# GpSimd loads the first batch's values, and a new order of the startup, in an attention and two-layer expert kernel

## The chip, the cores and the metric

The kernel runs on one core of a Trainium2 chip. The metric is device time in microseconds (us) of one execution; lower is better. PE is the matrix engine (TensorE), DVE VectorE, ACT ScalarE, POOL GpSimd, SP SyncE, which here only issues transfers.

## What is computed

The reference, cut to its core (B=4, H=8, S=576, D=64, 32 packed queries per head, 2304 tokens, model width 512, hidden width 2048, all float32):

```python
def sm_attn(qq, kk, vv):
    s = scale * qq @ kk.T
    a = exp(s - max(s)); a = a / (sum(a) + 1e-9)
    return a @ vv
p_packed = sm_attn(p, k, v)          # 32 rows per head
x = sm_attn(q, p_packed, p_packed)   # 576 rows per head
x = x.transpose(0, 2, 1, 3).reshape(2304, 512)
h = x @ w1_in;  x = (h * tanh(softplus(h))) @ w1_out      # Mish
h = x @ w2_in;  out = (where(h > 0, h, exp(min(h,0)) - 1)) @ w2_out   # ELU
```

## The kernel before

The program has three stretches. `startup()` does the attention of batch 0 and 1, decodes the first layer's weights and runs the first 32 hidden tiles of both; `mixture1` does the rest of the first layer with the attention of batches 2 and 3 beside it; `mixture2` does the second layer. The change touches `startup()` alone.

In `startup()` the order on PE, DVE, ACT and SP is written out by hand. First come fixed lines: `make_identity(nc, ident)` on POOL (a memset, then an affine select that puts the ones on the diagonal), two memsets of the buffers `words` on POOL, the copy `one` of `ident`, then on PE six `busy()` and 35 `brief()` matmuls of `one` that compute nothing that is used. Behind them stand the loads of batch 0's keys `k` (four, SP and ACT in turn), of the packed queries `p` (four small ones) and of the values `v` (`load_vt`, eight). Then the string `ORDER` is played from left to right; each name appends one step's instructions to its engines' queues. POOL isn't in the set of engines whose order is kept: its queue is ordered by the planner of the framework, which looks at when an instruction could start.

The names that matter, for batch 0 (leading 0):

- `lq00` to `lq03` load the queries (SP and ACT in turn); `r0`, `r1`, ... load a raw weight tile (512 KB, on SP).
- `0k0` to `0k3` turn the keys on DVE (line 409), `tp0` the packed queries (line 1085); `0A0`, `0A1` are the first scores on PE (line 441).
- `0M` (row maximum, DVE), `0E` (exp, ACT, line 468), `0R` (sum and reciprocal, DVE, lines 480 and 483), `0T` (turn on PE, line 495), `0V` (copy out of PSUM), `0K` (times the values, PE, line 520; needs all eight value loads), `0P` (scaled by the reciprocal, line 537), `0U` (turn, PE, line 552), `0W` (copy out of PSUM into `pt`; `@` puts a step on ACT in place of DVE).
- `0q0` to `0q3` turn the queries on DVE (line 409); `0S0` is the second scores' matmul (line 574), `0t0`, `0t1` its turn on DVE (line 603), `0X`, `0Y`, `0N`, `0B`, `0H`, `0L` the second softmax and the splitting of its result into `a2h` and `a2l`.
- `dN.0` to `dN.5` decode weight tile N: `.0` and `.2` on ACT (lines 199, 201, 206, 209), `.1` and `.3` on DVE (lines 221 or 217, and 237), `.4` issues the store of a finished pair on POOL (line 245).
- `w` and `x` are more unused matmuls on PE; `f00` folds the attention into the weights, `g0` is the first matmul of the first layer.

The values' loads of batch 0 in `load_heads` go by two pieces, partitions 0 to 63 with five blocks (1,280 bytes in one run) and 64 to 127 with four (1,024 bytes), two heads each: `(eng if b or not j else nc.scalar).dma_start(...)`, where `eng` is SP. So SP and ACT issue four each.

Of the kernel before, what the change touches and what calls it, by code (L numbers as in the profile page):

```python
# [40 lines left out]


ORDER = """
0k0 lq00 0k1 lq01 lq02 0k2 0k3 lq03 tp0 0A0 r0 0A1 0M0 r1 0E0 0M1 r2 0E1 w w w w w w w w w w w w w
0T0 0R0 0V0@ 0T1 0R1 r3 w w w w 0K0 r4 0V1@ r5 0q0 0K1 0P0@ r6 0q1 0U0 0P1@ 0q2 r7 0q3 0U1 0W0@ r8
d0.0 0W1 w w w w w 0S0 d0.1 r9 d0.3 d0.4 d1.0 0t0 0t1 d1.1 d1.3 d1.4 r10 d2.0 d2.2 r11 0X2 d3.0 0X1
0Y2 r12 0N2 d4.0 d4.2 r13 0X0 0Y1 d5.0 0B2 0Y0 d2.1 d2.4 0H2 0N0 r14 d6.0 0L2 0B0 r15 0X3 0H0 d7.0
0L0 0Y3 r16 d3.1 d7.2 d4.1 d8.0 d3.3 d3.4 r17 d4.4 d7.1 x x x x x x x x x x x x x x x x x x x x x x x
x x x x x x x x x x x x x x x x x z z z z f00 d9.0 d8.1 d4.5 d9.2 d8.3 d8.4 fh001 fh000 lk12 d9.1
d9.4 d10.0 fl000 d10.2 lk10 fl001 d11.0 d10.1 d10.4 x x x x x g0 d11.2 lk13 d6.1 d12.0 d5.1 g1 d11.1  # L50
d11.4 m0 lk11 d6.3 f01 d5.3 m1 pr1 0N1 g2 h0 h1 fh011 g3 l0 m2 fl011 fh010 G0 h2 l1 d5.4 fl010 d13.0
r18 d5.5 g4 lw100 l2 r19 0B1 m3 G1 m4 0N3 d6.4 d12.2 d6.5 r20 g5 d13.2 h3@ d12.1 G2 h4 m5 l3 d7.4 l4
r21 d12.4 d7.5 g6 d15.0 r22 d12.5 G3 r23 d13.1 m6 0B3 0H1 d13.4 h5@ 0L1 g7 0H3 d13.5 d14.0 G4 0L3 h6@
1k3 d14.2 l5 g8 m7 r24 l6 d15.2 d14.1 G5 h7 d15.1 m8 r25 d14.4 l7 d15.4 g9 d14.5 h8 d15.5 d16.0 G6
1k0 m9 l8 d19.0 tp1 g10 G7 1k1 m10 r26 h9 1k2 d19.2 l9 g11 d16.2 h10@ y7.0 d20.0 1A0 l10 r27 y7.1
y7.2 m11 g12 y7.3 d18.0 1M0 G8 d19.1 d19.4 m12 1E0 d18.1 g13 d20.1 G9 h11@ d18.3 d18.4 d17.0 l11 1R0
1A1 d16.1 d16.4 d17.2 d20.3 h12 G10 d17.1 d17.4 lv11 d25.0 l12 d26.0 1M1 d20.4 lv12 g14 d23.0 d25.1
d20.5 G11 1E1 lv10 d26.1 d25.3 d25.4 d24.0 lv13 1R1 f02 m13 d23.1 d24.1 d26.3 d26.4 G12 d24.3 d24.4
m14 r28 fh021 r29 h13@ fh020 h14@ g15 l13 d21.0 l14 G13 fl020 r30 m15 fl021 d27.0 h15@ d21.1 g16
d22.0 l15 G14 d27.1 d21.3 d22.2 d27.3 d27.4 g17 d28.0 r31 d21.4@ lw101 f03 d22.1 m16 d21.5 m17 h16  # L60
g18 h17@ fh031 d22.4@ fh030 l16 G15 fl031 m18 d30.0 d28.1 g19 fl030 y15.2@ y15.1 h18 1T1 y15.3@ d22.5
m19 g20 y15.0@ l17 d30.2 1V1 G16 m20 d28.3 d31.0 d30.1 g21 d31.2 d28.4@ h19@ 1T0 l18 d29.0 l19 g22
d28.5 m21 1V0 G17 d29.2 m22 d31.1 d23.3 1K0 h20@ d23.4 d31.4@ g23 l20 1P0@ lq11 d23.5 G18 m23 d31.5
d29.1 lq10 d30.4@ 1U0 d29.4@ G19 1W0 h21@ d29.5 l21 1K1 d30.5 h22 l22 G20 1P1@ lq12 1q1 1U1 h23@ G21
1W1 lq13 l23 1q0 g24 G22 m24 h24@ l24 1q2 g25 G23 m25 h25@ l25 1q3 g26 y23.0 1S0 y23.3 m26 y23.2 h26
g27 y23.1 1t0 G24 m27 l26 1S1 h27 G25 l27 1t1 1X0 g28 G26 m28 1X1 1Y0 g29 h28@ l28 G27 1Y1 1N0 m29
g30 1N1 G28 h29 m30 h30 f10 l29 1B0 G29 1B1 1H0 l30 fh101 1L0 fh100 g31 fl101 1H1 fl100 m31 1L1 h31
l31
"""


# [1 line left out]
def kernel(  # L73
# [12 lines left out]
    nc = tc.nc  # L86
# [49 lines left out]
    ident = const.tile([128, 128], F32, name="ident")  # L136
# [217 lines left out]
    def load_heads(src, dst, b, g, nm, eng):  # L354
        home = small if b else slot
        if nm == "v":
            t = home([128, 2, 5, D], F32, f"{nm}{b}_{g}")
            x = src[b, 2 * g:2 * g + 2].rearrange("h (p i) d -> p h (i d)", i=9)
            for r, j, n in RUNS:
                (eng if b or not j else nc.scalar).dma_start(  # L360
                    out=t[r:r + 64, :, 0:n, :].rearrange("p h i d -> p h (i d)"),
                    in_=x[:, :, D * j:D * (j + n)],
                )
        elif b == 0 or nm == "k" and b == 1:

            t = home([128, S // 32, 32], F32, f"{nm}{b}_{g}")
            ins = eng.dma_start(
                out=t.rearrange("p c d -> p (c d)"),
                in_=src[b, 2 * g:2 * g + 2].rearrange("h (t j) d -> (h t) (j d)", t=64),
            )  # L370
            if b == 1:
                tc.keep_in_program_order(ins)
        else:
            t = home([128, S // 32, 32], F32, f"{nm}{b}_{g}")
            for h in range(2):
                for x in range(2):
                    r = 64 * h + 32 * x
                    if nm == "q":
                        eng.dma_start(
                            out=t[r:r + 32],  # L380
                            in_=src[b, 2 * g + h, :, 32 * x:32 * x + 32].rearrange("(c t) d -> t c d", t=32),
                        )
                    for s in range(2 if nm == "k" else 0):
                        eng.dma_start(
                            out=t[r:r + 32, s * NB // 2:(s + 1) * NB // 2, :],
                            in_=src[b, 2 * g + s, h * HALF:(h + 1) * HALF, 32 * x:32 * x + 32].rearrange(
                                "(c t) d -> t c d", t=32
                            ),
                        )
# [549 lines left out]
    def load_kt(src, dst, b, kt, nm, eng=nc.sync):  # L939
        for gg in range(2):  # L940
            load_heads(src, dst, b, 2 * kt + gg, nm, eng)
# [43 lines left out]
    def startup():  # L985
# [11 lines left out]
        for x in words:  # L997
            z = sg.tile([128, 1024], I32, tag="sg", name="words")
            nc.gpsimd.memset(z, 0)
            x.extend((z[:, 0:512], z[:, 512:1024]))  # L1000
        if WARM:
            wu = ps_h.tile([128, 512], F32, tag="h", name="warm")

            one = const.tile([128, 128], F32R, name="one")
            nc.gpsimd.tensor_copy(out=one, in_=ident)

            def busy():
                nc.tensor.matmul(
                    out=wu.rearrange("p (r n) -> p r n", r=4), lhsT=one,
                    rhs=one.rearrange("p (r n) -> p r n", r=1).to_broadcast([128, 4, 128]),  # L1010
                )

            def brief(m, n):
                nc.tensor.matmul(out=wu[0:m, 0:n], lhsT=one[:, 0:m], rhs=one[:, 0:n])

            def gated():
                x = A2h[0][:, 0, 0, :]
                nc.tensor.matmul(out=wu[:, 0:HALF], lhsT=x[:, 0:128], rhs=x)

            for i in range(WARM):  # L1020
                busy()
            for i in range(P["BRIEF"]):
                brief(32, 64)
        for g in range(4):
            load_heads(k, kt_in, 0, g, "k", (nc.sync, nc.scalar)[g % 2])
# [14 lines left out]
        for b in range(2):  # L1040
            for g in range(4):
                step(f"{b}k{g}", transpose_heads(kt_in, kT, b, g, "kT")[0])
                step(f"{b}q{g}", transpose_heads(qt_in, qT, b, g, "qT")[0])
                for nm, src, dst in (("k", k, kt_in), ("v", v, vt_in), ("q", q, qt_in)):
                    eng = nc.sync if b or g % 2 else nc.scalar
# [223 lines left out]
    with tc.manual_schedule(engines={e.engine for e in (nc.tensor, nc.vector, nc.scalar, nc.sync)}):  # L1269
        startup()  # L1270
# [32 lines left out]
```

## Time and the profile before

| | |
|---|---|
| median of 3 runs | 776.6 us (776.24 to 778.09) |
| profiled execution, its own time | 775.32 us |
| its span, first to last instruction | 773.5 us |
| PE busy, share of the span | 756.9 us, 98% |
| DVE, ACT, POOL busy | 528.7, 397.6, 104.5 us |
| mean granted clock of PE | 0.998 |

The span is 1.8 us shorter than the execution's own time. PE is busy nearly throughout, but in the first 40 us much of that is unused matmuls, so the stretch has to be read by its chain of waits, engine by engine.

### The profile page before, as it was taken

What the parts mean: (1) busy time and instruction counts of PE and PEld (TensorE: products, weight loads), DVE (VectorE), ACT (ScalarE), POOL (GpSimd) and SP (SyncE); (2) the same over time, 40 slices, a digit from 0 to 9 for tenths busy, and PEclk for the clock granted to TensorE, in tenths of its full rate; (3) what the DMA queues carried; (4) which work ended last, traced back from release to release, by engine and by line L of the source; (5) the groups of instructions that cost most, each with busy time, mean ns of one, the idle gap of its engine ahead of it and who ended that gap; (6) DMA issues with size and microseconds to landing.
All of it is one profiled execution on the core that took longest, in us unless ns stands there. A gap on an engine that the chain in (4) does not pass through costs nothing.

```text
span 773.5 us, 14181 instructions
## 1 busy us (share of the span) xinstructions
PE 756.9 (98%) x5276; PEld 679.0 (88%) x5276; DVE 528.7 (68%) x1132; ACT 397.6 (51%) x843; POOL 104.5 (14%) x199
## 2 busy tenths in 40 slices
PE   8899999999999999999999999999999999999997
PEld 6598898898889988999988889888998999899986
DVE  5999977735853679877667788866455686445554
ACT  3899826573657467665545344534323354223323
POOL 1100000120120215661000003133000001000000
PEclk9999999999999999999999999999999999999999
DMA  8998646685583555777666235456343347333312
GB/s 290 412 367 271 171 126 177 203 230 157 129 268 56 151 194 191 262 254 238 219 220 201 100 109 199 155 197 198 108 120 119 103 140 243 108 110 116 129 55 82
DMA packets 95108, 138.82 MB, mean 179 GB/s; under 512 B 57920, under 2 KB 63616, under 8 KB 95040
## 3 DMA queue, kind: packets, MB, share of 16 engines
q1 hardware_dynamic: 83104, 105.73, 44.1%
q0 software_dynamic: 10208, 29.90, 10.6%
q10 hardware_dynamic: 1728, 2.29, 0.9%
q8 instruction: 42, 0.69, 0.3%
q14 instruction: 26, 0.21, 0.1%
HBM read 109.58 MB, written 28.31 MB: 178 GB/s over the span
## 4 chain that ended last, share of the span: by engine, by line
PE 84%; ACT 6%; DVE 4%; DMA 3%; issue 2%; POOL 0%; SPq 0%; ACTq 0%; DVEq 0%; POOLq 0%
PE h L833 22%; PE o L913 8%; PE o L915 8%; PE o L914 8%; PE acc L738 7%; PE acc L737 7%; PE acc L739 7%; PE h L701 3%; PE h L702 3%; PE h L703 3%; DMA raw_w1o<-in_moe_w_out_dram 1%; PE pm L667 1%; PE pm L520 1%; DMA w_dr<-w2c 1%; ACT words L206 1%
## 5 line engine op out<-in xcount | busy, mean ns | idle before, releaser
L833 PE MATMUL h<-y,w2c 128*128 128x384 f32 x1008 | 198.1, 338 | 1.8 <-ACT hs L397 1.2
L833 PEld LDWEIGHTS h<-y,w2c 128*128 128x128 f32 x1008 | 179.5, 188 | 13.4 <-ACT hs L397 2.0
L738 PE MATMUL acc<-gl,w1oh 128*128 128x288 f32 x512 | 151.2, 296 | 0.4 <-DVE gl L719 0.3
L739 PE MATMUL acc<-gh,w1ol 128*128 128x288 f32 x512 | 150.3, 295 | 0.0
L737 PE MATMUL acc<-gh,w1oh 128*128 128x288 f32 x512 | 148.7, 296 | 0.2 <-ACT gh L397 0.2
L913 PE MATMUL o<-w2oh,gh 128*128 128x512 f32 x288 | 113.5, 394 | 0.0
L914 PE MATMUL o<-w2ol,gh 128*128 128x512 f32 x288 | 112.6, 391 | 0.0
L915 PE MATMUL o<-w2oh,gl 128*128 128x512 f32 x288 | 101.1, 393 | 0.0
L738 PEld LDWEIGHTS acc<-gl,w1oh 128*128 128x128 f32 x512 | 96.1, 188 | 5.3 <-issue 2.3
L737 PEld LDWEIGHTS acc<-gh,w1oh 128*128 128x128 f32 x512 | 95.0, 188 | 6.2 <-issue 4.5
L739 PEld LDWEIGHTS acc<-gh,w1ol 128*128 128x128 f32 x512 | 96.0, 188 | 1.2 <-issue 0.8
L719 DVE TENSOR_TENSOR gl<-t,gh 128x288 fp32r<-128x288 f32 x128 | 57.2, 451 | 43.3 <-ACT gh L397 42.4
L711 ACT ACTIVATE t<-h 128x288 f32<-128x288 f32 x128 | 51.0, 404 | 55.9 <-PE h L703 53.0
L701 PE MATMUL h<-a2h,gh 128*128 128x288 f32 x256 | 76.9, 301 | 1.3 <-ACT t L711 0.9
L326 POOL DMA_DIRECT2D w_dr<-w2c x112 | 59.7, 539 | 135.7 <-DVE w2c L272 126.9
L703 PE MATMUL h<-a2h,gl 128*128 128x288 f32 x256 | 76.1, 298 | 0.3 <-DVE gl L272 0.3
L702 PE MATMUL h<-a2l,gh 128*128 128x288 f32 x256 | 75.8, 296 | 0.0
L264 ACT ACTIVATE gh<-t 128x384 fp32r<-128x384 f32 x96 | 50.1, 522 | 48.8 <-DVE t L844 47.5
L270 DVE TENSOR_TENSOR gl<-t,gh 128x384 fp32r<-128x384 f32 x96 | 53.1, 554 | 15.8 <-ACT gh L264 15.4
L914 PEld LDWEIGHTS o<-w2ol,gh 128*128 128x128 f32 x288 | 54.1, 188 | 9.4
L913 PEld LDWEIGHTS o<-w2oh,gh 128*128 128x128 f32 x288 | 54.0, 187 | 9.4 <-ACT gh L264 0.5
L397 ACT ACTIVATE gh<-t 128x288 fp32r<-128x288 f32 x112 | 49.2, 442 | 24.1 <-PE acc L739 22.1
(139 smaller groups left out, 1095.2 us busy)
## 6 DMA issues: line engine op xcount, KB each, us to landing
w2c<-w_dr SPq DMA_DIRECT2D x84, 512.0 KB, 3.6
w_dr<-w2c POOLq DMA_DIRECT2D x112, 128.0 KB, 3.1
w1r<-w_dr SPq DMA_DIRECT2D x24, 512.0 KB, 5.7
raw_w1i<-in_moe_w_in_dram SPq DMA_DIRECT2D x16, 512.0 KB, 10.8
raw_w1o<-in_moe_w_out_dram SPq DMA_DIRECT2D x16, 512.0 KB, 9.1
raw_w2i<-in_moe_w_in_dram SPq DMA_DIRECT2D x16, 512.0 KB, 4.8
raw_w2o<-in_moe_w_out_dram SPq DMA_DIRECT2D x16, 512.0 KB, 3.6
y_dr<-y POOLq DMA_DIRECT2D x16, 288.0 KB, 4.9
```

The source lines that it names most:

```text
L326: nc.gpsimd.dma_start(out=w2_dr[n // 2][:, n % 2, p], in_=d[x][:, i].bitcast(F32))
L701: nc.tensor.matmul(out=hp, lhsT=wh, rhs=xh, start=(kt == 0), stop=False)
L702: nc.tensor.matmul(out=hp, lhsT=wh, rhs=xl, start=False, stop=False)
L703: nc.tensor.matmul(out=hp, lhsT=wl, rhs=xh, start=False, stop=(kt == 1))
L719: nc.vector.tensor_tensor(out=gl, in0=d["t"], in1=gh.bitcast(F32), op=ALU.subtract)
L737: nc.tensor.matmul(out=o, lhsT=wh[:, cs], rhs=gh, start=first, stop=False)
L738: nc.tensor.matmul(out=o, lhsT=wh[:, cs], rhs=gl, start=False, stop=False)
L739: nc.tensor.matmul(out=o, lhsT=wl[:, cs], rhs=gh, start=False, stop=last)
L833: nc.tensor.matmul(out=hp, lhsT=w[:, p, a, :], rhs=y[:, b, :], start=start and p == 0 and i == 0, stop=p == 1 and i == 2, skip_group_check ...
L913: nc.tensor.matmul(out=o, lhsT=gh[:, ts], rhs=wh, start=(n == 1), stop=False)
L914: nc.tensor.matmul(out=o, lhsT=gh[:, ts], rhs=wl, start=False, stop=False)
L915: nc.tensor.matmul(out=o, lhsT=gl[:, ts], rhs=wh, start=False, stop=(n == NK))
```

## The change

The eight value loads of batch 0 are issued by POOL. Since they are gone from SP and ACT, the query loads stand next in those two queues behind the keys and the packed queries. The copy `one` moves from POOL to DVE. In `ORDER`, `0q0` and `0q1` move ahead of `0R0`, `0q2` and `0q3` each come some steps earlier, `0W0` moves from ACT to DVE, and the turn of the second scores (`0t0`, `0t1`) comes behind the DVE steps of weight tile 1. The rest of `ORDER` is the same, though its lines break at other places.

```diff
-0k0 lq00 0k1 lq01 lq02 0k2 0k3 lq03 tp0 0A0 r0 0A1 0M0 r1 0E0 0M1 r2 0E1 w w w w w w w w w w w w w
-0T0 0R0 0V0@ 0T1 0R1 r3 w w w w 0K0 r4 0V1@ r5 0q0 0K1 0P0@ r6 0q1 0U0 0P1@ 0q2 r7 0q3 0U1 0W0@ r8
-d0.0 0W1 w w w w w 0S0 d0.1 r9 d0.3 d0.4 d1.0 0t0 0t1 d1.1 d1.3 d1.4 r10 d2.0 d2.2 r11 0X2 d3.0 0X1
+0k0 lq00 0k1 lq01 lq02 0k2 0k3 lq03 tp0 0A0 r0 0A1 0M0 r1 0E0 0M1 r2 0E1 0q0 w w w w w w w w w w w w
+w 0T0 0q1 0R0 0V0@ 0T1 0R1 r3 w w w w 0K0 r4 0V1@ r5 0q2 0K1 0P0@ r6 0q3 0U0 0P1@ r7 0U1 0W0 r8 d0.0
+0W1 w w w w w 0S0 d0.1 r9 d0.3 d0.4 d1.0 d1.1 d1.3 d1.4 0t0 r10 d2.0 0t1 d2.2 r11 0X2 d3.0 0X1 0Y2
...
             for r, j, n in RUNS:
-                (eng if b or not j else nc.scalar).dma_start(
+                (eng if b else nc.gpsimd).dma_start(
...
             one = const.tile([128, 128], F32R, name="one")
-            nc.gpsimd.tensor_copy(out=one, in_=ident)
+            nc.vector.tensor_copy(out=one, in_=ident)
```

## Rows read from the trace of the kernel before

**Rows 1.** Timeline from the start: start, us, engine, line, operation [idle before <-releaser].
```profile
0.88 1.84 POOL L999 MEMSET words<- 128x1024 int32 x2
2.75 0.28 POOL masks.py:199 TENSOR_SCALAR_AFFINE_SELECT ident<-ident 128x128 f32<-128x128 f32 x1
3.10 0.29 POOL L1005 CAST one<-ident 128x128 fp32r<-128x128 f32 x1
...
3.44 2.93 PE L1008 MATMUL warm<-one 128*128 128x512 f32 x6 [3.44 <-POOL one L1005]
...
7.14 0.40 DVE L1085 STREAM_TRANSPOSE pT<-pr 128x256 f32<-128x256 f32 x1
...
8.17 2.58 PE L441 MATMUL pm<-kT,pT 32*32 32x288 f32 x64
```

**Rows 2.** Timeline of SP's transfer issues; us covers all in the row.
```profile
4.45 3.25 SPq L360 DMA_DIRECT2D v<-in_v_dram  x4
7.82 2.18 SPq L367 DMA_DIRECT2D q<-in_q_dram  x2
10.07 3.50 SPq L162 DMA_DIRECT2D raw_w1i<-in_moe_w_in_dram  x4
```

**Rows 3.** Timeline from the reciprocals to the second softmax, three engines.
```profile
13.22 0.21 DVE L480 TENSOR_SCALAR rs<-sm 128x1 f32<-128x1 f32 x1 [0.55 <-ACT e L468]
13.80 1.44 DVE L409 STREAM_TRANSPOSE qT<-q 128x576 f32<-128x576 f32 x2 [0.17 <-DMA q<-in_q_dram]
14.33 1.73 PE L520 MATMUL pm<-v,a1t 128*32 128x64 f32 x80
15.30 0.31 ACT L537 ACTIVATE pv<-pm,rs 128x64 f32<-128x64 f32 x1 [0.51 <-PE pm L520]
16.13 0.31 ACT L537 ACTIVATE pv<-pm,rs 128x64 f32<-128x64 f32 x1 [0.52 <-PE pm L520]
17.46 0.43 DVE L399 COPY pt<-pm 64x256 f32<-64x256 f32 x1
17.65 0.68 ACT L199 ACTIVATE raw_w1i<-raw_w1i 128x512 f32<-128x512 f32 x1 [0.59 <-DMA raw_w1i<-in_moe_w_in_dram]
18.36 0.43 DVE L221 TENSOR_SCALAR w1v<-raw_w1i 128x512 int32<-128x512 int32 x1 [0.47 <-ACT raw_w1i L199]
19.66 1.58 DVE L603 STREAM_TRANSPOSE x<-pm 128x288 f32<-128x288 f32 x4
21.16 0.39 DVE L221 TENSOR_SCALAR w1v<-raw_w1i 128x512 int32<-128x512 int32 x1
22.18 0.45 DVE L615 TENSOR_REDUCE mx<-x 128x9 f32<-128x288 f32 x1
```

**Rows 4.** Busy time by stretch: length, PE, PEld, DVE, ACT, POOL, clock, DMA, GB/s.
```profile
19.60:28.80 9.20, 9.20 (x40) 7.34 (x40) 8.80 (x24) 5.90 (x12) 0.68 (x1) 1.00 1.02 413
...
39.40:60.00 20.60, 20.52 (x151) 20.10 (x152) 19.33 (x43) 19.98 (x44) 0.00 (x0) 1.00 0.98 370
```

**Rows 5.** Tile q up to 30 us: its four loads, issue to landing.
```profile
DMA to landing us min/median/max: 5.7/6.2/7.1
```

**Rows 6.** Timeline of POOL's transfer issues.
```profile
32.25 0.99 POOL L245 DMA_DIRECT2D w_dr<-w1v  x1 [8.99 <-DVE w1v L237]
...
295.48 7.44 POOL L326 DMA_DIRECT2D w_dr<-w2c  x14 [14.67 <-DVE w2c L272]
```

**Rows 7.** Transfers issued from 295 to 303 us: KB each, median us to landing.
```profile
w_dr<-w2c POOLq DMA_DIRECT2D x14, 128.0 KB, 2.2
```

**Rows 8.** The same from 154 to 158 us.
```profile
w_dr<-w2c POOLq DMA_DIRECT2D x2, 128.0 KB, 6.0
```

**Rows 9.** Queues from 27 to 28 us: packets, MB, share of 16 engines.
```profile
q0 software_dynamic: 54, 0.22, 53.8%
q1 hardware_dynamic: 53, 0.19, 47.1%
```

**Rows 10.** POOL's queue from 109 to 114 us (two stores `y_dr`, 256 rows of 2,304 bytes).
```profile
q0 software_dynamic: 160, 0.59, 36.6%
```

More of the change, by code (lines that the diff above doesn't have):

```diff
@@ L43 @@
 ORDER = """
-0k0 lq00 0k1 lq01 lq02 0k2 0k3 lq03 tp0 0A0 r0 0A1 0M0 r1 0E0 0M1 r2 0E1 w w w w w w w w w w w w w
-0T0 0R0 0V0@ 0T1 0R1 r3 w w w w 0K0 r4 0V1@ r5 0q0 0K1 0P0@ r6 0q1 0U0 0P1@ 0q2 r7 0q3 0U1 0W0@ r8
-d0.0 0W1 w w w w w 0S0 d0.1 r9 d0.3 d0.4 d1.0 0t0 0t1 d1.1 d1.3 d1.4 r10 d2.0 d2.2 r11 0X2 d3.0 0X1
-0Y2 r12 0N2 d4.0 d4.2 r13 0X0 0Y1 d5.0 0B2 0Y0 d2.1 d2.4 0H2 0N0 r14 d6.0 0L2 0B0 r15 0X3 0H0 d7.0
-0L0 0Y3 r16 d3.1 d7.2 d4.1 d8.0 d3.3 d3.4 r17 d4.4 d7.1 x x x x x x x x x x x x x x x x x x x x x x x
@@ L49 @@
[L49 to L68, printed above, removed]
+0k0 lq00 0k1 lq01 lq02 0k2 0k3 lq03 tp0 0A0 r0 0A1 0M0 r1 0E0 0M1 r2 0E1 0q0 w w w w w w w w w w w w
@@ new lines @@
+w 0T0 0q1 0R0 0V0@ 0T1 0R1 r3 w w w w 0K0 r4 0V1@ r5 0q2 0K1 0P0@ r6 0q3 0U0 0P1@ r7 0U1 0W0 r8 d0.0
+0W1 w w w w w 0S0 d0.1 r9 d0.3 d0.4 d1.0 d1.1 d1.3 d1.4 0t0 r10 d2.0 0t1 d2.2 r11 0X2 d3.0 0X1 0Y2
+r12 0N2 d4.0 d4.2 r13 0X0 0Y1 d5.0 0B2 0Y0 d2.1 d2.4 0H2 0N0 r14 d6.0 0L2 0B0 r15 0X3 0H0 d7.0 0L0
+0Y3 r16 d3.1 d7.2 d4.1 d8.0 d3.3 d3.4 r17 d4.4 d7.1 x x x x x x x x x x x x x x x x x x x x x x x x x
+x x x x x x x x x x x x x x x z z z z f00 d9.0 d8.1 d4.5 d9.2 d8.3 d8.4 fh001 fh000 lk12 d9.1 d9.4
@@ new lines @@
+d10.0 fl000 d10.2 lk10 fl001 d11.0 d10.1 d10.4 x x x x x g0 d11.2 lk13 d6.1 d12.0 d5.1 g1 d11.1 d11.4
+m0 lk11 d6.3 f01 d5.3 m1 pr1 0N1 g2 h0 h1 fh011 g3 l0 m2 fl011 fh010 G0 h2 l1 d5.4 fl010 d13.0 r18
+d5.5 g4 lw100 l2 r19 0B1 m3 G1 m4 0N3 d6.4 d12.2 d6.5 r20 g5 d13.2 h3@ d12.1 G2 h4 m5 l3 d7.4 l4 r21
+d12.4 d7.5 g6 d15.0 r22 d12.5 G3 r23 d13.1 m6 0B3 0H1 d13.4 h5@ 0L1 g7 0H3 d13.5 d14.0 G4 0L3 h6@ 1k3
+d14.2 l5 g8 m7 r24 l6 d15.2 d14.1 G5 h7 d15.1 m8 r25 d14.4 l7 d15.4 g9 d14.5 h8 d15.5 d16.0 G6 1k0 m9
@@ new lines @@
+l8 d19.0 tp1 g10 G7 1k1 m10 r26 h9 1k2 d19.2 l9 g11 d16.2 h10@ y7.0 d20.0 1A0 l10 r27 y7.1 y7.2 m11
+g12 y7.3 d18.0 1M0 G8 d19.1 d19.4 m12 1E0 d18.1 g13 d20.1 G9 h11@ d18.3 d18.4 d17.0 l11 1R0 1A1 d16.1
+d16.4 d17.2 d20.3 h12 G10 d17.1 d17.4 lv11 d25.0 l12 d26.0 1M1 d20.4 lv12 g14 d23.0 d25.1 d20.5 G11
+1E1 lv10 d26.1 d25.3 d25.4 d24.0 lv13 1R1 f02 m13 d23.1 d24.1 d26.3 d26.4 G12 d24.3 d24.4 m14 r28
+fh021 r29 h13@ fh020 h14@ g15 l13 d21.0 l14 G13 fl020 r30 m15 fl021 d27.0 h15@ d21.1 g16 d22.0 l15
@@ new lines @@
+G14 d27.1 d21.3 d22.2 d27.3 d27.4 g17 d28.0 r31 d21.4@ lw101 f03 d22.1 m16 d21.5 m17 h16 g18 h17@
+fh031 d22.4@ fh030 l16 G15 fl031 m18 d30.0 d28.1 g19 fl030 y15.2@ y15.1 h18 1T1 y15.3@ d22.5 m19 g20
+y15.0@ l17 d30.2 1V1 G16 m20 d28.3 d31.0 d30.1 g21 d31.2 d28.4@ h19@ 1T0 l18 d29.0 l19 g22 d28.5 m21
+1V0 G17 d29.2 m22 d31.1 d23.3 1K0 h20@ d23.4 d31.4@ g23 l20 1P0@ lq11 d23.5 G18 m23 d31.5 d29.1 lq10
+d30.4@ 1U0 d29.4@ G19 1W0 h21@ d29.5 l21 1K1 d30.5 h22 l22 G20 1P1@ lq12 1q1 1U1 h23@ G21 1W1 lq13
@@ L69 @@
+l23 1q0 g24 G22 m24 h24@ l24 1q2 g25 G23 m25 h25@ l25 1q3 g26 y23.0 1S0 y23.3 m26 y23.2 h26 g27 y23.1
+1t0 G24 m27 l26 1S1 h27 G25 l27 1t1 1X0 g28 G26 m28 1X1 1Y0 g29 h28@ l28 G27 1Y1 1N0 m29 g30 1N1 G28
+h29 m30 h30 f10 l29 1B0 G29 1B1 1H0 l30 fh101 1L0 fh100 g31 fl101 1H1 fl100 m31 1L1 h31 l31
 """
```

## The prediction

> **What bounds the kernel now.** I read four views, from the whole to the place. The table of engines comes first: PE is busy 98% of the span, so the long middle is PE's, and a change confined to the first 25 us can only move the whole rest earlier or later by a fixed amount. The busy time by stretch comes second, and shows what carries such a shift on. From 19.6 to 28.8 us VectorE works 8.80 of 9.20 us, while PE's 40 matmuls there are all unused ones; from 39.4 to 60 us ScalarE works 19.98 of 20.60 us [rows 4]. So behind 20 us first VectorE and then ScalarE has a full queue, and PE takes over behind them: an advance or delay of VectorE at 22 us passes on one for one.
>
> The timeline of the first 20 us comes third: what sets the start of that full queue? PE starts at 3.44 us, released by `one` on POOL, and works through its unused matmuls until the first scores at 8.17 us. Keys and packed queries were turned earlier: the last turn starts at 7.14 us and ends at 7.54, 0.63 us ahead of those scores [rows 1]. So up to the scores the chain is POOL's `ident` and `one`, then PE's own queue. From there it is scores, exp, turn, values at 14.33 us, scaling at 15.30 and 16.13, the copy of `pt` on VectorE at 17.46, the second scores, and their turn on VectorE at 19.66 us [rows 3]. Neither queries nor values are seen holding that chain. The queries hold only their own turns (a wait of 0.17 us at 13.80), and these lie beside the chain.
>
> The fourth view, the issues of the transfers, tells why weights come late: SP issues four value loads from 4.45, two query loads from 7.82 and the first weight tile only at 10.07 us [rows 2]. ScalarE waits 0.59 us for that tile and starts it at 17.65; VectorE waits 0.47 us for ScalarE and takes it at 18.36 [rows 3]. These are the gaps that the change can close.
>
> **Values on POOL.** SP's query loads move from 7.82 to 4.45, where the first value load stood, 3.37 us earlier, and the first weight tile from 10.07 to 6.70 [rows 2]. POOL pays eight issues. Fourteen such issues back to back took 7.44 us, 0.53 each; the slowest row shows 0.99 [rows 6]. Behind the affine select (end 3.03 us [rows 1]) the first starts at 3.1 and the last at 3.1 + 7 x 0.53 = 6.8 us, or at 10.0 with 0.99 each. POOL has nothing else to do there. Landing: POOL's transfers of this size (128 KB) took 2.2 us on a quiet queue and 6.0 beside a busy one [rows 7, 8]. That gives 9.0 to 12.8 us, and 16.0 with slow issue too. The values are needed at 14.33 us. I take 12.8, hidden with 1.5 us to spare; each us beyond 14.33 would be paid in full.
>
> The loads also share the transfer engines with weights that now start sooner. Where both kinds of queue have work, packets go one for one: 54 of POOL's to 53 of SP's in one us [rows 9]. So the size of a packet decides. POOL's queue joins short rows: 256 rows of 2,304 bytes went as 160 packets, 3.7 KB in the mean with the small closing ones [rows 10]. The values are 4 x (160 + 128) KB = 1.18 MB, some 320 such packets, 320 / 54 = 5.9 us even if SP's queue always has work; from 3.1 + 2.2 = 5.3 us that ends at 11.2. Unjoined they are 1,024 pieces and 19 us, ending at 24.3; that is a rival below.
>
> The Trainium skill ("DMA: Bandwidth & Descriptors", section Queues, rings and completion order) states the first half of this: each transfer engine takes turns between queues by whole packets. This trace agrees (54 to 53). The sum would be the same by the rule and by the row.
>
> What the values' new early traffic takes from keys and packed queries is covered by the 0.63 us before the scores [rows 1]. The nearest measure of how much later a load gets is the spread of landing between equal loads, 7.1 - 5.7 = 1.4 us for the queries [rows 5]; so the loss lies between 0 and 1.4 - 0.63 = 0.8 us. I take 0, since the values' first packets can't come before 5.3 us and the packed queries were issued before 4.45.
>
> **The copy `one` on VectorE.** POOL's took 0.29 us. No row shows this shape on VectorE; the nearest are 0.21 (one element per row) and 0.43 (256 columns) [rows 3]. So PE starts 0.08 earlier to 0.14 later. I take 0. VectorE has nothing else then.
>
> **Query turns ahead of the reciprocals.** Two turns take 1.44 us. With loads from 4.45 us and at most 7.1 us to landing [rows 2, 5], the first query lands at 11.6, the second, issued about a us later, at 12.6. The turns end near 13.4. Each reciprocal with its sum takes 0.58 us by the starts at 13.22 and 13.80 [rows 3], so both end at 14.6, needed at 15.30: 0.7 us to spare. ScalarE's scaling would queue behind a later one, and PE's turn behind that, one for one. The other two turns, 1.44 us, end at 16.0; `0W0` on VectorE (0.43) then stands where VectorE is free, and `0W1` waits for PE as before. Cost 0. ScalarE is free behind 16.13 + 0.31 = 16.44 us [rows 3].
>
> **Weights ahead of the scores' turn.** This is where the gain is. With the tile issued at 6.70 us, ScalarE can decode it at 16.44, not 17.65; its 0.68 us end at 17.12, ahead of the copy of `pt`, which ends at 17.89. VectorE then goes straight on: tile 0's pair, tile 1's pair, 1.02 us each by the starts at 21.16 and 22.18, to 19.93. That is 0.27 later than the scores' turn started before, so PE's second scores are hidden. The turns take 21.16 - 19.66 = 1.50, to 21.43 us. The second softmax starts there, not at 22.18 [rows 3]: 0.75 us earlier. The other bound is the one gap that a row names in full, 0.47 us. I take 0.6.
>
> **Sum.** 0.6 us earlier at 22 us, all else hidden, and passed on whole: 775.32 - 0.6 = 774.7 us for the profiled execution. The median of the runs shown is 1.3 us above that execution, so on the median's scale 776.6 - 0.6 = **776.0 us**. This measurement tells about 0.3%, 2.3 us, from no change, so I forecast no measurable difference.
>
> **Rivals.**
>
> *The loads delay `ident` (slower).* POOL's order isn't the program's: both memsets of `words` ran ahead of the affine select, which stands before them in the code [rows 1]. The value loads wait for nothing, so they can slip in at the same place. Each one ahead puts off `one`, PE's start and the first scores by 0.53 us. Eight make 4.25, less the 0.6: 776.6 + 3.65 = 780.3 us. It takes six of eight to be slower by over 2.3 us. Against it: the affine select waited for one short memset only, and two memsets, not more, were there to fill that. Chance 0.14 for six or more.
>
> *The values come late (slower at its far end).* Slow issue and slow landing give 16.0 us, 1.7 late: 776.6 + 1.7 - 0.6 = 777.7. Unjoined packets give up to 24.3 us, 10 late. It is slower by over 2.3 us from a landing at 17.2 on. Joining and the middle of the rows speak against it. Chance 0.10, half of it beyond 17.2. The Trainium skill ("SBUF — State Buffer", section SBUF: two separate sides) has a rule that would make it so: while VectorE copies float32 within SBUF in its two-port mode, POOL can't write its descriptors, and a 620 ns transfer took 3,100. No row here shows such a stall as long; by its figure eight loads would need some 25 us, an estimate from that page. VectorE's work at 4.5 to 7.5 us is turns, and `one` is the only such copy.
>
> *The weights were the bound (faster).* If what holds the first 60 us is the supply of weights, 3.37 us earlier is worth 3.4: 773.2 us. For it: the transfer engines' share is 1.02 and 0.98 in both stretches. Against: VectorE and ScalarE are full there [rows 4], so they aren't kept waiting. Chance 0.08.
>
> *Nothing arrives.* ScalarE's full queue from 39 us may start by something else than VectorE; then 0.6 us is lost, 776.6 us. Chance 0.10.
>
> **How the numbers follow.** The forecast has 0.58, and by itself spans 775.8 to 777.4 (0.75 gained to 0.8 lost). Faster by over 0.3% holds the third rival and a little of the forecast's tail, 0.10; slower the first, half of the second and a little, 0.18; the same 0.72. The range reaches to the first and third rival and stops short of them: 774.0 to 779.4 us.
>
> **What would show it.** On POOL eight issues from 3.1 us directly behind the affine select, and PE's first matmul still at 3.4; before it, the first rival. First scores at 8.2 and values' matmul at 14.3, else the values or keys came late. Query issues at 4.5 and the first weight issue near 6.7. No wait of VectorE between the copy of `pt` and the second softmax, which starts near 21.5. The same 0.6 us at every later stage; if it is gone at 60 us, the last rival holds. The prediction fails if POOL's queue is ordered otherwise, or if the values' packets are not joined.

## The result, and the profile after

The changed kernel takes **781.44 us** (median of 6 runs, 780.28 to 784.06) beside 776.72 us (776.24 to 779.04, 6 runs) for the kernel before: ratio **1.0057**, 95% interval 1.0042 to 1.0071. It is slower by 0.6%, more than the 0.3% that tells a change from none, and outside the range of 774.0 to 779.4 us. Its profiled execution took 780.60 us with a span of 778.8, 5.3 us more than the span before.

The page of the changed kernel: the span, busy time by engine, and the granted clock in 40 slices.

```profile
span 778.8 us, 14194 instructions
PE 760.5 (98%) x5276; PEld 681.3 (87%) x5276; DVE 529.0 (68%) x1134; ACT 396.8 (51%) x842; POOL 108.9 (14%) x206
PEclk9799999999999999999999999999999999999999
```

The busy times are those of before to within a few us. What is new is the 7 in the second slice of the clock, 19.5 to 38.9 us; everything lost lies at or before it.

The chain of waits of the changed kernel up to 45 us (start, us, what) shows the place. Before, no value load stood on the way to the values' matmul at 14.33 us; now the last of eight does.

```profile
2.75 0.28 POOL ident masks.py:199
3.04 4.18 POOL v L359 x7
7.22 9.97 DMA v<-in_v_dram
17.19 0.14 issue
17.33 2.82 PE pm L519 x80
```

The timeline of the changed kernel, beside [rows 1 to 3]:

```profile
3.00 4.84 POOL L359 DMA_DIRECT2D v<-in_v_dram  x8
3.07 0.23 DVE L1004 CAST one<-ident 128x128 fp32r<-128x128 f32 x1 [3.07 <-POOL ident masks.py:199]
3.35 2.93 PE L1007 MATMUL warm<-one 128*128 128x512 f32 x6 [3.35 <-DVE one L1004]
4.56 3.02 SPq L366 DMA_DIRECT2D q<-in_q_dram  x2
7.63 1.87 SPq L161 DMA_DIRECT2D raw_w1i<-in_moe_w_in_dram  x4
8.29 0.45 DVE L1084 STREAM_TRANSPOSE pT<-pr 128x256 f32<-128x256 f32 x1
8.79 1.95 PE L440 MATMUL pm<-kT,pT 32*32 32x288 f32 x64 [0.71 <-DVE pT L1084]
...
17.33 2.82 PE L519 MATMUL pm<-v,a1t 128*32 128x64 f32 x80 [2.92 <-DMA v<-in_v_dram]
17.39 1.44 DVE L408 STREAM_TRANSPOSE qT<-q 128x576 f32<-128x576 f32 x2 [3.54 <-DMA q<-in_q_dram]
18.83 0.32 ACT L536 ACTIVATE pv<-pm,rs 128x64 f32<-128x64 f32 x1 [4.04 <-PE pm L519]
...
26.13 1.58 DVE L602 STREAM_TRANSPOSE x<-pm 128x288 f32<-128x288 f32 x4 [1.08 <-PE pm L573]
27.62 0.41 DVE L614 TENSOR_REDUCE mx<-x 128x9 f32<-128x288 f32 x1
44.20 0.71 ACT L710 ACTIVATE t<-h 128x288 f32<-128x288 f32 x2
```

Two things happen. The values' matmul starts at 17.33 us, not 14.33 [rows 3]: +3.00. Then the way from it to the second softmax, 7.85 us before (14.33 to 22.18), takes 10.29 (17.33 to 27.62): another 2.44, though nothing on that way waits for a transfer any more. The matmul itself took 2.82 us instead of 1.73. The softmax is 5.44 later; the first activation of the expert layers (at 38.99 us before) is 5.20 later and the end 5.28: the middle of the kernel passes the delay on.

Busy time by stretch of the changed kernel (length, PE, PEld, DVE, ACT, POOL, clock, DMA share, GB/s) names the second thing:

```profile
14.40:17.30 2.90, 0.00 (x1) 0.00 (x1) 0.00 (x0) 0.39 (x2) 0.00 (x0) 1.00 1.02 358
18.40:28.60 10.20, 10.20 (x135) 6.23 (x136) 5.86 (x14) 3.48 (x7) 0.58 (x1) 0.51 1.03 408
28.60:39.40 10.80, 10.29 (x59) 7.75 (x58) 10.49 (x26) 8.69 (x18) 0.85 (x1) 1.00 1.03 413
```

PE stands idle for 2.9 us, and the granted clock behind that falls to 0.51, the 1.2 GHz level, for some 10 us. In the kernel before PE is busy throughout the first of these stretches, and its clock in the second is 1.00. The transfer engines, at 1.02 of their time, are full while PE waits: the values aren't late for want of traffic, but stand in a line. From 14 to 17 us that traffic is SP's (87.8% of the engines' time); what PE waits for is the tail of the values, 31 packets of 384.

Tile v of the changed kernel, its issues by line and its landing:

```profile
L359 POOL DMA_DIRECT2D v<-in_v_dram x8: 594/602/742, 3.0 to 7.2; - x8
DMA to landing us min/median/max: 5.1/7.5/10.0
```

In the kernel before, the same eight took 2.9 to 5.4 us from issue to landing, the last at 12.85 us. Tile q of the changed kernel, which had taken 5.7 to 7.1 us before [rows 5]:

```profile
DMA to landing us min/median/max: 5.5/8.9/10.5
```

The first weight tile, issued 2.44 us earlier (7.63 for 10.07), landed at 18.67 us, 1.04 *later* than before (17.63). The kernel before shows why there was nothing to win in the line; its stretch from 8 to 14 us:

```profile
8.00:14.00 6.00, 5.80 (x94) 4.29 (x92) 2.68 (x9) 2.68 (x10) 0.00 (x0) 1.00 0.98 297
```

The transfer engines were taken for 0.98 of that time already. By this reading an earlier issue could change the order of the loads there, but hardly the end of the last of them.

### The profile page after: what moved, and what is told of

It reads as the page before. It is cut to its first block, busy times and chain, and to the rows that moved or that the text cites. A ratio compares the mean times of both kernels' runs of the same rounds, so it can differ in the third digit from the quotient of the medians.

```text
span 778.8 us, 14194 instructions
## 1 busy us (share of the span) xinstructions
PE 760.5 (98%) x5276; PEld 681.3 (87%) x5276; DVE 529.0 (68%) x1134; ACT 396.8 (51%) x842; POOL 108.9 (14%) x206
## 3 DMA queue, kind: packets, MB, share of 16 engines
q0 software_dynamic: 10592, 31.08, 11.2%
## 4 chain that ended last, share of the span: by engine, by line
PE 82%; ACT 5%; DVE 5%; DMA 4%; issue 2%; POOL 1%; SPq 0%; ACTq 0%; DVEq 0%; POOLq 0%
PE h L832 22%; PE o L912 8%; PE o L914 8%; PE o L913 8%; PE acc L737 7%; PE acc L736 7%; PE acc L738 7%; PE h L700 3%; PE h L701 3%; PE h L702 3%; DMA v<-in_v_dram 3%; PE pm L666 1%; PE pm L519 1%; DMA w1r<-w_dr 1%; PE pm L588 1%
```

## The experiments

Ten kernels ran beside the changed one, two of them twice: twelve runs. "Changed" is the kernel after the change. A time of a whole run is the median of its executions; a time of a single step is from one profiled execution.

**1. The loads alone.** The kernel before with only the new load line; `one` stays on POOL, behind the eight issues.

```diff
-                (eng if b or not j else nc.scalar).dma_start(
+                (eng if b else nc.gpsimd).dma_start(
```

> Theory A (the values come late because, issued by POOL, they share the transfer engines with queries that now stand next in SP's and ACT's queues): moving the eight loads alone, with the old ORDER and `one` on POOL, brings the whole loss and a little more, since the 1.0 us that the new place of the weights' steps wins is not there: values' matmul near 17.3 us as in the changed kernel, first TensorE clock drop there too, 782 to 783.5 us. Theory B (the new ORDER makes the loss, for example DVE's wait for late query turns): within 0.3% of before, 775.5 to 778 us.

780.17 us, ratio 1.0053 (1.0032 to 1.0073). The timeline of this kernel:

```profile
7.80 0.31 POOL L1005 CAST one<-ident 128x128 fp32r<-128x128 f32 x1
8.16 2.93 PE L1008 MATMUL warm<-one 128*128 128x512 f32 x6 [8.16 <-POOL one L1005]
18.46 1.73 PE L520 MATMUL pm<-v,a1t 128*32 128x64 f32 x80
26.31 0.45 DVE L615 TENSOR_REDUCE mx<-x 128x9 f32<-128x288 f32 x1
42.98 0.71 ACT L711 ACTIVATE t<-h 128x288 f32<-128x288 f32 x2
```

PE starts 4.7 us late, so its whole queue is late and it meets values that have landed (last issue about 7.2 + 8.9 = 16.1 us). It doesn't idle, its clock in 18.40 to 28.60 us is 1.00, and from matmul to softmax it needs 7.85 us, as before. So the loads alone bring a loss, but not in the way that theory A expected (matmul near 17.3 us and a low clock).

**2. The loads and `one`.** As 1, with `one` on DVE.

```diff
-            nc.gpsimd.tensor_copy(out=one, in_=ident)
+            nc.vector.tensor_copy(out=one, in_=ident)
```

> The eight loads on POOL and `one` on DVE, with the old ORDER. Theory C with the clock: PE starts at 3.35, values' matmul near 17.3 after a wait of some 3 us, the clock falls, and the 1.0 us that the weights' new place won in the changed kernel is missing: first activation 6 to 6.5 us later than before, 782 to 783.5 us, so slower than the run in which `one` stayed on POOL (780.2), where PE's unused matmuls started late and covered the wait. Rival (the new ORDER has its own part in the loss): 779 to 781 us.

783.03 us, ratio 1.0064 (1.0046 to 1.0083): the interval overlaps that of run 1. Timeline and stretch of this kernel:

```profile
17.43 3.16 PE L520 MATMUL pm<-v,a1t 128*32 128x64 f32 x80 [3.11 <-DMA v<-in_v_dram]
29.09 0.45 DVE L615 TENSOR_REDUCE mx<-x 128x9 f32<-128x288 f32 x1
45.64 0.71 ACT L711 ACTIVATE t<-h 128x288 f32<-128x288 f32 x2
```

```profile
16.00:18.00 2.00, 0.57 (x15) 0.60 (x19) 0.90 (x2) 0.00 (x0) 0.00 (x0) 0.54 1.01 385
18.40:28.60 10.20, 10.20 (x152) 6.21 (x144) 3.55 (x9) 3.85 (x8) 0.00 (x0) 0.61 1.03 409
```

The pair 1 and 2 separates clock from lateness. Here the values' matmul starts 1.03 us *earlier* than in 1 (17.43 to 18.46), but PE had waited 3.11 us, its clock is at the lower level, and the first expert activation is 2.66 us *later*.

**3. The order alone.** The changed kernel with the old load line: values on SP and ACT.

```diff
-                (eng if b else nc.gpsimd).dma_start(
+                (eng if b or not j else nc.scalar).dma_start(
```

> Values back on SP and ACT ahead of the queries, the new ORDER and `one` on DVE kept. Theory A: values' matmul back near 14.4 us, no drop of the clock; the first query lands near 13.7 as before, so the two query turns ahead of the reciprocals hold these until about 15.8 and the first scaling moves from 15.30 to about 15.9: 0.6 us lost, 776.7 to 777.7 us. Theory B: the loss stays, 780 to 782 us.

777.84 us, ratio 1.0016 (1.0000 to 1.0031). The values' matmul is on time at 14.09 us. The query turns, now ahead of the reciprocals, wait 2.90 us for their loads; the first scaling comes at 16.38 us (15.30 before), the second softmax at 22.48 (22.18 before), the first expert activation at 39.17. So without the loads the order is worth nothing.

**4. PE kept busy.** The changed kernel with 23 more unused matmuls `w` ahead of the values' matmul.

```diff
-... 0R1 r3 w w w w 0K0 ...
+... 0R1 r3 w w w w w w w w w w w w w w w w w w w w w w w w w w w 0K0 ...
```

> The changed kernel with 23 more unused 128x128 matmuls ahead of the values' matmul, 0.128 us each, so that PE works through the 2.9 us in which it waited. Theory A1 (half of the loss is the clock, which fell to 0.5 for 10.24 us after PE stood still): values still land near 17.2 us, but the granted clock stays at 1.00, the scores' turn starts near 22.7 and not at 26.1, and 3.4 us come back: 777.5 to 778.5 us. Rival (the lateness alone costs all, and the low clock lies beside other waits): 781 us as the changed kernel, whatever the clock.

780.62 us, ratio 1.0057 (1.0029 to 1.0085). Timeline and stretch of this kernel:

```profile
18.28 2.06 PE L519 MATMUL pm<-v,a1t 128*32 128x64 f32 x80 [1.27 <-DMA v<-in_v_dram]
25.97 0.41 DVE L614 TENSOR_REDUCE mx<-x 128x9 f32<-128x288 f32 x1
42.53 0.71 ACT L710 ACTIVATE t<-h 128x288 f32<-128x288 f32 x2
```

```profile
18.40:28.60 10.20, 10.20 (x181) 7.55 (x180) 7.71 (x20) 5.35 (x11) 0.58 (x1) 1.00 1.03 409
```

The values' matmul starts 0.95 us later than in the changed kernel, with the clock at 1.00 behind it, and the softmax comes 1.65 *earlier*: 7.69 us on the way instead of 10.29. That is the price of the low clock, 2.60 us. The time of the whole doesn't show it: its ratio is that of the changed kernel, and its median misses the 777.5 to 778.5 us expected. This profiled execution (784.28 us) lost 5.5 us more between 190 and 240 us, where ScalarE waited 5.22 us for a weight store, and four of the ten executions have a mean granted clock of 0.992 or 0.993, as the changed kernel has (0.992). A second profile of the same kernel follows below.

**5. Queries behind the values.** The changed kernel with batch 0's queries on POOL too, behind the values; the query turns stand in `ORDER` where they stood before.

```diff
+                    if nm == "q" and not b:
+                        eng = nc.gpsimd
```

> The changed kernel with batch 0's queries issued by POOL too, behind the values, and the query turns in the old places. Theory A2 (it is the queries that took the values' turn): values land by about 12.5 us, their matmul starts near 14.4 with no wait, the clock stays; the queries then come by about 16 to 17.5 us, so the time is 775.5 to 778 us. Rival A3 (POOL's queue is slow by itself, or gives way to the weight tiles that SP now issues from about 4.5 us): the values land no earlier than 16 us, the queries after them, 781 us or more.

784.79 us, ratio 1.0110 (1.0083 to 1.0136), the slowest. The queries were out of the way, but SP's weights came in their place. A timeline row of this kernel, and its queues from 12 to 17 us (packets, MB, share of 16 engines):

```profile
18.70 1.41 PE L520 MATMUL pm<-v,a1t 128*32 128x64 f32 x32 [4.29 <-DMA v<-in_v_dram]
```

```profile
q1 hardware_dynamic: 183, 0.67, 54.6%
q0 software_dynamic: 184, 0.55, 44.8%
```

One packet of SP's for each of POOL's. The theory that queries are what delays the values falls: whatever SP has queued takes every second turn.

**6. Queries and weights held back.** The changed kernel with batch 0's query tiles in the keys' buffers, so that their loads wait for the keys' turns, and SP's weights behind them.

```diff
-            t = home([128, S // 32, 32], F32, f"{nm}{b}_{g}")
+            if nm == "k" and b == 0:
+                ktile[g] = home([128, S // 32, 32], F32, f"{nm}{b}_{g}")
+            t = ktile[g] if b == 0 else home([128, S // 32, 32], F32, f"{nm}{b}_{g}")
```

> The changed kernel with each query load written into the tile of the keys it follows, so that it (and the weights behind it on SP) can't start before those keys are turned, 5.1 to 8.4 us: the values on POOL have the transfer engines nearly to themselves until about 8 us. Theory C (the values come late only because, on POOL, they are no longer served ahead of the queries and weights but take turns with them): values' matmul back to 14.0 to 15.0 us, no clock drop, first activation of the first layer within 1 us of before's 39.0, total 775.5 to 778 us. Rival D (POOL's transfers are slow by themselves, whatever stands beside them): the values' matmul stays at 16.5 us or later, 779 us or more.

783.08 us over 10 runs, from 776.5 to 786.9; ratio 1.0069 (1.0046 to 1.0092). The profiled execution was the shortest one, 776.5 us: it shows what the edit does to the values, not why the median is high. Tile v, and the queues from 6 to 8 us, of this kernel:

```profile
DMA to landing us min/median/max: 5.1/5.9/8.0
```

```profile
q0 software_dynamic: 148, 0.45, 96.7%
```

With the line nearly to themselves for 2 us the values move 0.45 MB in it, land by about 7.2 + 8.0 = 15.2 us, and their matmul starts at 15.36. (The profile names the reciprocal on VectorE as what released it; that ended at 15.30, and the last load landed at 15.23, so both came at once.) That is two of the three us. So their place in the line is the cause of most of the delay. The third us is not explained by it.

On record is also the mean granted clock of every execution: 0.990 to 0.996 in the seven of 781.2 us and more, 0.998 to 1.000 in the three below. So a low clock goes with the long executions; where it fell in them no profile shows.

**7. Values of one head pair on POOL, the rest on SP and ACT.** The changed kernel with the query turns in their old places.

```diff
-                (eng if b else nc.gpsimd).dma_start(
+                (eng if b else nc.gpsimd if g == 0 else nc.sync if not j else nc.scalar).dma_start(
```

> A version meant to win: two of the eight value loads on POOL from 3.0 us, six on SP and ACT ahead of the queries as before, `one` on DVE, the query turns in their old places, the scores' turn behind weight tile 1. Theory C: the six are served first, the two have the engines to themselves until 5 us, so the values are in time; queries and weights come 0.5 to 0.8 us earlier than before, which lets the new place of the weights' steps win 0.3 to 0.6 us at the first activation: 776 us, not to be told from before by time. Rival D: the two on POOL land last and late, first activation over 0.5 us later than before.

777.60 us, ratio 1.0005 (0.9994 to 1.0017), no difference. The values' matmul starts at 13.75 us, the softmax at 22.02, the first expert activation at 38.94 us. Two loads on POOL cost nothing, and win nothing.

**8. The order without the query turns.** The kernel before with `one` on DVE, `0W0` on DVE and this part of `ORDER` alone:

```diff
-... d0.4 d1.0 0t0 0t1 d1.1 d1.3 d1.4 r10 d2.0 d2.2 r11 ...
+... d0.4 d1.0 d1.1 d1.3 d1.4 0t0 r10 d2.0 0t1 d2.2 r11 ...
```

> All loads as before, `one` on DVE, the query turns in their old places, only the scores' turn behind weight tile 1 and the copy of `pt` on DVE new. The run with the whole new ORDER lost 1.3 us at the scores' turn to the query turns' wait and won 1.0 us behind it. Here the wait is gone, but weight tile 1 lands near 18.9 us as before, so the scores' turn waits for its decode to about 20.7: first activation 0.3 us earlier to 0.2 later than before, 776 to 777.5 us.

777.86 us, ratio 1.0000 (0.9988 to 1.0012). Rows of this kernel:

```profile
15.97 2.76 DVE L409 STREAM_TRANSPOSE qT<-q 128x576 f32<-128x576 f32 x4 [3.32 <-DMA q<-in_q_dram]
18.65 0.83 DVE L399 COPY pt<-pm 64x256 f32<-64x256 f32 x2
19.08 2.37 PE L574 MATMUL pm<-qT,pt 32*32 32x288 f32 x64 [1.52 <-DVE pt L399]
21.77 1.58 DVE L603 STREAM_TRANSPOSE x<-pm 128x288 f32<-128x288 f32 x4
```

The values' matmul starts at 13.52 us. The expectation that the wait is gone fails: the query turns waited 3.32 us for their loads in this execution and hold the copy of `pt`, now on VectorE too, until 18.65 (17.46 before). From there VectorE works without a gap through `pt` and both weight tiles, and the scores' turn slips to 21.77 (19.66 before). PE waited 1.52 us for `pt`, and its clock fell to 0.5 from 20.67 to 24.08 us. The first expert activation comes at 39.85 us, 0.86 later than before, and outside what was expected; the time of the whole is that of before.

**9. Held back, with twelve more `w`.** Kernel 6 with cover for a wait of some 1.5 us.

```diff
-... 0R1 r3 w w w w 0K0 ...
+... 0R1 r3 w w w w w w w w w w w w w w w w 0K0 ...
```

> The kernel whose queries wait for the keys' turn, with 12 more unused 128x128 matmuls (1.5 us) ahead of the values' matmul. That kernel's profiled execution took 776.5 us and its others up to 786.9. Theory E (its long executions are those in which the values land a little later, PE stands still for long enough and the clock falls): the matmuls cover the wait, the values' matmul starts near 16 us, the median comes to 777.5 to 779 us and nearly all executions lie below 781. Rival F (the spread comes from the middle of the kernel, where stores of w2c and loads decide): the median stays at 781 to 784 us.

782.74 us, ratio 1.0055 (1.0034 to 1.0076). The values landed at 17.2 us this time, PE waited 2.10 behind its cover, and the clock in 18.40 to 28.60 us was 0.67. The cover was too short. The median lies where rival F put it, 781 to 784 us, but with the wait uncovered the run doesn't decide between E and F; its executions above and below 781 us don't differ in their mean clock (0.992 to 0.999 and 0.996 to 0.999, the longest, 790.78 us, at 0.990).

**10 and 11. Kernels 6 and 4 profiled a second time,** without a further edit.

> A second look at the kernel whose queries wait for the keys, unchanged, to see where one of its longer executions loses its time. Theory E: if it takes over 781 us, its values' matmul starts at 16 us or later and the granted clock shows 0.5 for about 10 us behind that. Rival F: the first activation is within 1 us of 39.6 us, and the loss appears behind 190 us.

> A second look at the changed kernel with 23 more unused matmuls, unchanged; its first profiled execution (784.3 us) lost 3.5 us up to the first activation and 5.5 more between 190 and 240 us, where ScalarE waited 5.2 us for a store. If that second loss belongs to single executions, this one takes 778 to 780 us with the same 3.5 at the first activation; if it belongs to the kernel, 783 us or more.

779.37 and 780.39 us, one execution each. Kernel 6 again: matmul at 15.64, softmax 23.31, first expert activation at 40.54, and the end 3.85 us late: 1.5 us up to that activation, 1.2 more between 350 and 410 us. This wasn't one of its executions over 781 us, so theory E isn't tested by it. Kernel 4 again: matmul at 17.81, softmax 25.49, first expert activation at 42.00, and the end 5.06 us late; so most of the 5.5 us lost in mid-kernel belonged to the one execution, but 1.7 of it came here too.

**12. One packet of program code.** The trace's records of the 16 transfer engines show why the landing varies. Of each load, every engine reports its part; of the last value load (us):

```
kernel          8th report  15th   16th   code packet (16 KB): start, us
changed         15.25       16.30  17.19  14.93, 1.22
4               16.11       16.38  18.15  15.30, 1.27
4, second       16.03       16.53  17.67  15.15, 1.30
9               15.43       15.64  17.17  14.89, 1.22
6               13.97       14.34  15.23  14.69, 1.14
6, second       15.08       15.34  15.51  14.79, 1.30
1               15.85       16.05  16.13  17.81, 1.11
2               15.63       16.89  17.29  14.98, 1.28
5               17.13       17.30  18.57  15.35, 1.33
```

In six of these nine one engine is 0.9 to 1.8 us behind the fifteen others, and a packet of program code holds one engine for over 1.1 us at about that time (in 2 the last is 0.4 behind, in the second profile of 6 it is 0.2). In 1 it came behind the landing, and the reports end together. The experiment: twelve more short matmuls ahead of the first scores, to move that packet.

```diff
-            for i in range(P["BRIEF"]):
+            for i in range(P["BRIEF"] + 12):
```

> The changed kernel with twelve more of the short unused matmuls ahead of the first scores (47 of 128x64 for 35; one is 0.057 us, so 0.7 us, which fit into the 0.71 us that PE waits there). In the changed kernel one packet of 16 KB of program code is read at 14.93 us and holds its transfer engine for 1.22 us; fifteen engines report the last value load done by 16.30 us and the last one at 17.19. In the run where that packet came at 17.81 us, behind the landing, the sixteen reports end within 0.1 us of each other (16.05 and 16.13). Theory F: the packet is read when PE has gone through some 130 matmuls with their weight loads; twelve more of them ahead move it to 12 to 13.5 us, the last report comes within 0.4 us of the one before it, the last value load lands at 16.2 to 16.6 and the values' matmul starts at 16.3 to 16.7, 0.6 to 1.0 earlier than in the changed kernel. The rest of its delay (2.0 to 2.4 us against 14.33) stays, and so PE's wait, the low clock or not. Theory G: one of the sixteen engines is late of itself (more packets of its own): the packet moves, but the last report still stands 0.9 us or more behind the fifteenth, and the values' matmul starts at 17.2 or later. Theory H: the packet doesn't depend on PE: it stays at 14.8 to 15.1 us.

782.92 us, ratio 1.0084 (1.0067 to 1.0101). The packet didn't move (14.80 us, 1.19 long), so it doesn't follow PE's count of matmuls. But the pattern stands, sharper: fifteen reports by 15.50 us, the sixteenth at 17.03, the matmul at 17.17. Its queues from 14 to 16 us:

```profile
q1 hardware_dynamic: 163, 0.61, 88.4%
q0 software_dynamic: 29, 0.05, 11.6%
q8 instruction: 1, 0.02, 3.7%
```

The records don't name a packet's engine, and no run moved the code packet alone, so that it is the cause isn't shown. But they give every packet's start and length. In 2, 4 (both profiles), 9 and 12 one of the values' last packets starts within 0.02 us of the end of the code packet (12: code until 15.99, the values' last closing packet at 15.98), as it would if that engine had been held. In 6 it wasn't that: the values' last packet started at 14.67 us, the code packet at 14.69. In the changed kernel the last one starts 0.23 us behind the code packet's end and in 5 1.1 us behind it, which leaves it open.

**All runs in one table** (us; clock in 18.40 to 28.60 us; "way" is from the values' matmul to the second softmax):

| kernel | values' matmul | PE waited for it | clock | way | first expert activation |
|---|---|---|---|---|---|
| before | 14.33 | - | 1.00 | 7.85 | 38.99 |
| 1 loads | 18.46 | - | 1.00 | 7.85 | 42.98 |
| 2 loads, `one` | 17.43 | 3.11 | 0.61 | 11.66 | 45.64 |
| changed | 17.33 | 2.92 | 0.51 | 10.29 | 44.20 |
| 4 busy | 18.28 | 1.27 | 1.00 | 7.69 | 42.53 |
| 4, second profile | 17.81 | 1.04 | 1.00 | 7.68 | 42.00 |
| 6 held back | 15.36 | 1.02 | 1.00 | 7.68 | 39.62 |
| 6, second profile | 15.64 | 1.25 | 1.00 | 7.67 | 40.54 |
| 9 held, busy | 17.30 | 2.10 | 0.67 | 10.01 | 43.83 |
| 12 code packet | 17.17 | 2.52 | 0.60 | 10.64 | 44.31 |
| 5 queries behind | 18.70 | 4.29 | 0.50 | 11.47 | 46.76 |
| 3 order | 14.09 | - | 1.00 | 8.39 | 39.17 |
| 7 two on POOL | 13.75 | - | 1.00 | 8.27 | 38.94 |
| 8 order, old turns | 13.52 | - | 0.83 | 9.75 | 39.85 |

With all values on POOL and the clock whole the way is 7.67 to 7.69 us by the new order and 7.85 by the old one (1; before too); with the clock low it is 10.0 to 11.7. In 3, 7 and 8, whose values' matmul is early, it is 8.3 to 9.8.

## Why the prediction was wrong

**The step that failed** is in "Values on POOL": "I take 12.8, hidden with 1.5 us to spare". The last value load landed at 17.2 us, 10.0 after its issue, where the nearest rows gave 2.2 to 6.0 [rows 7, 8]. Two mistakes stand behind it. The rows are of stores on a quiet queue or beside one busy one; here eight loads stood in line behind each other while two other queues had work, on transfer engines that were full before the change (0.98 from 8 to 14 us). And the estimate by packets was right in its first half only. Packets do go one for one where both queues have work (183 to 184 in run 5), as the Trainium skill has it ("DMA: Bandwidth & Descriptors", section Queues, rings and completion order); run 5's trace agrees. But 54 packets per us came from stores of 4 KB rows [rows 9], 16 x 0.538 us / 54 = 0.16 us of an engine for 4.1 KB. The values' packets, joined from short rows, took in run 6, over 2 us of 16 engines, 32 x 0.967 us / 148 = 0.21 us for 3.0 KB: 69 ns per KB for 39. And there were 384 of them, the small closing ones (4 bytes, a third of them) counted, where the prediction had 320. In the changed kernel 98 went from 5 to 8 us and 255 from 8 to 14, some 42 per us, with 56.3% of the engines' time beside 48.2% for the two other queues (the profile gives the engines 1.05 in all there). The last large one ended at 15.53 us, where the estimate had 11.2, and fifteen of sixteen engines reported by 16.30. Joining, on which the step rested, took place, but its packets were dear. The late sixteenth engine is the rest, 0.9 us (16.30 to 17.19), and no step had it.

The same line undid the premise that a load issued earlier lands earlier by as much ("With the tile issued at 6.70 us, ScalarE can decode it at 16.44"): the first weight tile landed 1.04 us later than before.

**What the prediction had no term for** is the clock. It priced a late landing "one for one": the second rival gave 777.7 us for 16.0, and called it slower from a landing at 17.2 on. At 17.2 the loss was 5.3 us of the span, not 2.3. By that price alone, 776.6 + 2.9 - 0.6 = 778.9 us, the late landing would have stayed inside the stated range; the clock took it out. The 5.44 us at the second softmax split, by the table, into +3.00 for the values, +2.60 for the low clock (10.29 against 7.69 in run 4) and -0.16 for the order (7.69 against 7.85). The total is measured; the split rests on run 4. The runs 1 and 2 show the clock's price a second way, 3.81 us by the old order (11.66 against 7.85). So the second rival, given a chance of 0.10, is the one that came, at its far end, but by neither of its ways: issue took 0.60 us each and the packets were joined.

**The other steps.**
- *A shift at 22 us passes on one for one*: right, 5.44 at the softmax, 5.28 at the end.
- *POOL's issues* from 3.1, 0.53 each, the last at 6.8: 3.00, 0.60 and 7.2. Right within 0.4 us. They were not ahead of `ident` (affine select at 2.75 us in both), so the first rival was wrong. (Run 1 shows what it feared one step on: with `one` left on POOL the eight issues run ahead of it, and PE starts at 8.16 us.) No issue took longer than 0.74 us. A stall of POOL's descriptors under VectorE's copies, which the Trainium skill describes ("SBUF — State Buffer", section SBUF: two separate sides), isn't in this trace.
- *Queries at 4.45, weights near 6.70*: 4.56 and 7.63. SP's query issues took 3.02 us (2.18 before).
- *Early traffic takes 0 from the keys and packed queries*: wrong in its size, harmless. The turn of the packed queries starts at 8.29 us (7.14), 1.15 later, and the first scores wait 0.71 us and start 0.62 later. Later unused matmuls are the cover: PE stands ready for the values at 14.40 us.
- *`one` on DVE*: 0.23 us, PE starts 0.09 earlier. Right.
- *Query turns ahead of the reciprocals, cost 0*: the first two turned at 11.82 us, the reciprocals end at 13.84. Right. The other two were to end at 16.0 and waited 3.54 us for their loads, until 17.39: hidden only because the values were later still.
- *Weights ahead of the scores' turn, gain 0.6*: at full clock the way got 0.16 us shorter (7.69 for 7.85), at low clock 1.0 to 1.4 (run 12 10.64, changed 10.29, run 2 11.66), each from single executions. With the values on their old queues nothing is left of it (runs 3 and 8). Right in sign, mis-sized, and smaller than the loss it was traded for. The reason given for it is not what happened: the first weight tile came later, not earlier.
- *The third rival*, supply of weights as the bound, finds no support: in run 5 the first weight tile was issued at 4.7 us and landed at 11.53, 6.1 earlier than before, and from the second softmax to the first expert activation it still took 16.59 us (16.81 before).

**What stays open.** Why a single packet of code falls at 14.7 to 15.4 us in the kernels with all values on POOL (17.8 in run 1, whose PE started late); why some executions of run 4 lose several us more in mid-kernel, where ScalarE waits for weight stores; where the long executions of run 6 lose theirs. Not run was the same place in the line on a hardware queue (the values on SP and ACT behind the queries), so how much of the delay is the place and how much POOL's own queue is known from run 6 alone. No version beat the kernel before: runs 3, 7 and 8 can't be told from it.

## What to carry to other kernels

A queue is a place in line: a load that stood ahead of others on its own queue competes with them packet by packet on another one, so price its landing by loads of the same row size beside the same neighbours, all of them counted. Where the transfer engines are already full, an earlier issue only changes the order. A wait of PE costs more than its length when the clock falls behind it (2.9 us of waiting, 2.6 more behind it here), so a wait that would be hidden "with 1.5 us to spare" needs a term for the case that it isn't, and unused matmuls to cover it help only if they reach to the landing. A step that looks free because it waits behind another late one (the query turns) must be priced again once that one is mended.

## What the runs showed of the hardware

- PE idle for 2.1 to 4.3 us (changed, 2, 5, 9, 12) went each time with a granted clock of 0.5, 1.2 GHz, for 7 to 14 us (the trace's clock records), which began between 1.3 us before the end of the wait (2) and 1.3 us behind it (9); after the waits of 1.0 to 1.3 us for the values (4, 6 and their second profiles) it was still 1.00 ten us on. Waits of 1.5 to 1.6 us went either way: one of 1.52 us in 8 was followed by 3.41 us at 0.5, and a wait of 1.55 to 1.56 us that most of these kernels have between 32 and 39 us was followed by the same 3.41 us in 1, 3, 7 and the second profile of 6, and by no fall in the kernel before, 2, 4, 6 and 9.
- POOL's queue joined rows of 1,280 and 1,024 bytes into packets of 5,120 and 4,096 bytes, 384 with the small closing ones for 1.18 MB. Per KB they took 1.75 times the time of the 4 KB stores (69 and 39 ns). By the trace's packet records one of four joined rows of 1,280 bytes took 0.326 us, and a single such row in the kernel before 0.073: four of them, 0.29, are no dearer than the joined packet.
- A landing waits for the slowest of 16 engines: in run 12 fifteen were done at 15.50 us and the sixteenth at 17.03.
- Program code comes over the same transfer engines: one packet of 16 KB took 1.1 to 1.3 us of one engine's time at 14.7 to 15.4 us (run 12: 14.80, 1.19).
